# One sum of the transform's first pass made by accumulating DMA transfers instead of VectorE

## The chip, the core and the metric

The kernel runs on one core of a Trainium2 chip. Its time is in device microseconds (us); the median of three runs stands for it. The engines are TensorE (PE in the profile), VectorE (DVE), ScalarE (ACT), GpSimd (POOL) and SyncE (SP). SP issues most transfers, ACT some stores; before the change POOL issues none.

## The reference

Four layers with residuals: two Fourier mixing layers and two attention layers with a memory. Only the first Fourier layer is touched here:

```python
a = jnp.einsum("bsd,ed->bse", x, dft_hid_re)
b = jnp.einsum("bsd,ed->bse", x, dft_hid_im)
y = jnp.einsum("ts,bse->bte", dft_seq_re, a) - jnp.einsum("ts,bse->bte", dft_seq_im, b)
...
x = x + _A_ref(_layernorm(x, axis=-1), A_dft_seq_re, A_dft_seq_im, A_dft_hid_re, A_dft_hid_im)
x = x + _B_ref(_layernorm(x, axis=-1), B_wq, B_wk, B_wv, B_wo, B_beta)
```

The sequence has 2048 rows of 512 features, all in float32. The kernel applies the sequence matrices first and the hidden ones after.

## The kernel before

**Tiling.** The 2048 output rows are four chunks (`tcn`, 0 to 3) of 512. The input rows are sixteen tiles of 128, taken in pairs (tile `k` and tile `k + 8`), so a chunk has eight steps, `k` = 0 to 7. For each chunk and step the array `ct` holds four 128x512 blocks of the sequence matrices, beside one another: the second and the first half of the real matrix, then the first and the second half of the imaginary one.

**Passes.** Chunk 0 goes the plain way (`contract`). Chunks 1 to 3 replace eight block products by seven, P1 to P7, of sums of blocks. A first pass runs P1, P2, P7 and P4 for chunks 1, 2 and 3, step by step, the four products in turn; a second pass runs P6, P5 and P3. Every float32 operand is split into a high and a low part, and each product is three matmuls (`matmul3`); with two output tiles a product's step is six matmuls, which the program calls a slot. A step of the first pass is four slots. When a product has run its eight steps, its two accumulators are read out into `c` (line 497 on ACT, line 499 on DVE).

**The step's operands** come from `read_all` (line 381), a generator placed at five slots ahead of the step's own slot `t`: -11, -6, -4, -2, -1. It takes two homes of 128x2x512 (`re` and `im`), fetches the four blocks into them, and makes three sums on DVE, one after another. With `re[0]`, `re[1]`, `im[0]`, `im[1]` the blocks in order:

- line 386: `im[0]` + `im[1]` replaces `im[0]`; it is P7's operand
- line 387: `re[1]` + the new `im[0]` replaces `im[1]`; it is stored in DRAM for the second pass (line 397, by ACT)
- line 390: `re[0]` + the new `im[1]` replaces `re[0]`, once `rights` has split the old `re`; it is P4's operand

The splits are lines 96 (ACT, the high part `chi`) and 98 (DVE, the low part `clo`). `chi` and `clo` have three buffers each, so a split waits until TensorE is through with an older one.

**Homes.** `raw_pair` hands out nine homes: four in `cring`, two in `craw`, three in `v_all`; always the one released longest ago. A step uses two. `release` only orders the program: on the chip a fetch into a home waits for the last reader of its old content, which for `im` is the store of line 397.

**Order.** Instructions keep their program order on TensorE; on DVE the sums are pinned to it (`pin`) and the rest is placed by a scheduler, which also orders SP's, ACT's and POOL's queues. Each engine runs its queue in order. `read_rest` (the second pass) is placed by slots too; its subtraction is line 409. `join_rows` changes the left operands (`xa`) between the passes.

Of the kernel before, what the change touches and what calls it, by code (L numbers as in the profile page):

```python
# [14 lines left out]
ALU = mybir.AluOpType  # L15
# [41 lines left out]
def spectral_infini_kernel(  # L57
# [13 lines left out]
    V, A, G, T = nc.vector, nc.scalar, nc.gpsimd, nc.tensor  # L71
# [18 lines left out]
    pin = tc.keep_in_program_order  # L90

    def split(hi, lo, src, scale=1.0, lo_engine=V, hi_engine=None):
        if hi_engine is V:
            return V.tensor_copy(hi, src), V.tensor_tensor(out=lo, in0=src, in1=hi.bitcast(F32), op=ALU.subtract)
        else:
            pin(A.activation(hi, src, AF.Copy, scale=scale))  # L96
        if scale == 1.0:
            lo_engine.tensor_tensor(out=lo, in0=src, in1=hi.bitcast(F32), op=ALU.subtract)  # L98
        else:
            V.scalar_tensor_tensor(  # L100
                lo, src, scale, hi.bitcast(F32), op0=ALU.mult, op1=ALU.subtract
            )
# [12 lines left out]
    def pair(name, tag, bufs, dtype=F32R):  # L115
        return sb.tile([P, 2, 512], dtype, name=name, tag=tag, bufs=bufs)
# [67 lines left out]
    def place(order, gen, *at):  # L184
        for t in itertools.chain(*at):
            slots.setdefault(t, []).append((order, gen))

    def run_from(t, n, step=1):
        return range(t, t + n * step, step)
# [14 lines left out]
    def place_spectral(x_in, x_out, t0, end, ln_at, direct):  # L204
# [69 lines left out]
        def change_rows(k):  # L274
            two, j = raw_pair()
            new = two[:, 0, : D // 2]
            fetch(new, joined[k][:, 0])
            yield
            replace(k, slice(D // 2, D), new)
            release(j)  # L280
            yield
# [34 lines left out]
        def raw_pair(own=False):  # L316
            clock[0] += 1
            if not homes:
                ring = sb.tile([P, 2 * LT, 512], F32, name="cring", tag="xT", bufs=1)
                homes.extend(ring[:, j : j + 2] for j in range(0, 2 * LT, 2))  # L320
                if direct:
                    homes.extend(pair("craw", "craw", 2, F32) for _ in range(2))
                    homes.extend(spare[:, j : j + 2] for j in range(0, 6, 2))
            elif not direct and len(homes) == LT and clock[0] > 24:
                homes.extend(pair("craw", "craw", 2, F32) for _ in range(2))
            j = min((j for j in range(LT if own else len(homes)) if released.get(j, 0) is not None), key=lambda j: released.get(j, 0))
            released[j] = None
            return homes[j], j

        def release(*held):  # L330
            for j in held:
                clock[0] += 1
                released[j] = clock[0]

        def rights(src):
            hi, lo = pair("chi", "chi", 3), pair("clo", "clo", 3)
            split(hi, lo, src)
            return [(hi[:, j], lo[:, j]) for j in range(2)]
# [8 lines left out]
        def fetch(dst, src):  # L347
            with tc.issue_after(last_stack[0].ins) if last_stack[0] else nullcontext():
                nc.sync.dma_start(dst, src)
# [31 lines left out]
        def read_all(tcn, k):  # L381
            (re, j), (im, n) = raw_pair(), raw_pair()
            fetch(re, ct[tcn, k, :, :2])
            fetch(im, ct[tcn, k, :, 2:])
            yield
            pin(V.tensor_tensor(out=im[:, 0], in0=im[:, 0], in1=im[:, 1], op=ALU.add))
            later.append(pin(V.tensor_tensor(out=im[:, 1], in0=re[:, 1], in1=im[:, 0], op=ALU.add)))
            yield
            right[tcn, "P2", k], right[tcn, "P1", k] = rights(re)
            pin(V.tensor_tensor(out=re[:, 0], in0=re[:, 0], in1=im[:, 1], op=ALU.add))  # L390
            yield
            hi, lo = pair("chi", "chi", 3), pair("clo", "clo", 3)
            split(hi[:, 0], lo[:, 0], im[:, 0])
            split(hi[:, 1], lo[:, 1], re[:, 0])
            right[tcn, "P7", k], right[tcn, "P4", k] = ((hi[:, h], lo[:, h]) for h in range(2))
            yield
            nc.scalar.dma_start(sums[tcn, k][:, 1], im[:, 1])
            release(j, n)
            yield
# [49 lines left out]
        def contract(tcn):  # L449
            ps = [[bank(f"u{d}") for d in range(DT)] for _ in range(2)]  # L450
            for k in range(HALF):
                for h2 in range(2):
                    for cc in range(2):
                        parts = right[tcn, cc, h2, k]
                        for d in range(DT):
                            matmul3(
                                ps[cc][d],
                                lambda h: xa[k + HALF * h2][:, h, d * P : (d + 1) * P],
                                lambda h: parts[h],
                                (k, h2) == (0, 0),  # L460
                                (k, h2) == (HALF - 1, 1),
                            )
                        if (k, h2, cc) != (HALF - 1, 1, 1):
                            yield
            for cc in range(2):
                for d in range(DT):
                    if d % 2 == 0:
                        block(tcn, (d // 2, cc))
                    dst = c[tcn, (d // 2, cc)][:, d % 2]
                    if cc == 0:  # L470
                        A.activation(dst, ps[cc][d], AF.Copy)
                    else:
                        V.tensor_scalar(dst, ps[cc][d], -1.0, None, op0=ALU.mult)
            yield
# [106 lines left out]
        t = start  # L581
        if direct:
            place(2, contract(0), run_from(t, 4 * HALF, 2))
            for k in range(HALF):
                place(3, read_plain(0, k), [t + 8 * k + d for d in (-12, -4, 1, 4)])
                place(3, change_rows(k), [t + 8 * k + d for d in (5, 9)])
            t += 8 * HALF
            names = "P1", "P2", "P7", "P4"
            for tcn in range(1, TC):
                for n, name in enumerate(names):  # L590
                    place(2, product(tcn, name), run_from(t + n, HALF, 4))
                for k in range(HALF):
                    place(3, read_all(tcn, k), [t + 4 * k + d for d in (-11, -6, -4, -2, -1)])
                t += 4 * HALF
            for k in range(HALF):
                place(3, join_rows(k), [t + 5 * k + d for d in (-33, -27)])
            for tcn in range(1, TC):
                for n, name in enumerate(CHAIN):
                    place(2, product(tcn, name), run_from(t + n, HALF, 3))
                for k in range(0, HALF, 2):  # L600
                    place(3, read_rest(tcn, k), [t + 3 * k + d for d in (-12, -6, -3, 0)])
                t += 3 * HALF
        else:
            for names in ("P1", "P7"), ("P2", "P4"):
                for tcn in range(TC):
                    for n, name in enumerate(names):
                        place(2, product(tcn, name), run_from(t + n, HALF, 2))
                    for k in range(HALF):
                        place(3, read_pair(tcn, k, names), [t + 2 * k + d for d in (-10, -6, -4, -3)])
                    t += 2 * HALF  # L610
            for k in range(HALF):
                place(3, add_rows(k), [t - 48 + 6 * k, t - 44 + 6 * k])
            for tcns in (0, 1), (2, 3):
                at = {tcn: [] for tcn in tcns}
                for name, tcn in itertools.product(CHAIN, tcns):
                    at[tcn] += run_from(t, HALF)
                    for k in range(0, HALF, 2):
                        place(3, read_two(tcn, k, name), [t + k + d for d in (-9, -4, -3)])
                    t += HALF
                for tcn in tcns:  # L620
                    place(2, chained(tcn), at[tcn])
        for k in range(2 * DT):
            cc, d = k // DT, k % DT
            tag = "craw" if k < 2 else ("chi", "clo")[k % 2]
            t = end - 7 + k if k < 2 else end - 3 + (k - 2) // 2
# [675 lines left out]
```

## Time and profile before

| | |
|---|---|
| median of 3 runs | 1825.14 us |
| lowest, highest | 1822.15, 1827.36 us |
| the profiled execution | 1827.82 us |
| its span | 1825.6 us |
| granted TensorE clock over the span | 0.991 |
| first pass, chunks 1 to 3 | 98 to about 230 us |
| second pass | to 338 us |
| runs of lines 386, 387, 390 | 24 each |

In the profile, PE is TensorE's matmuls and PEld its weight loads, which overlap. A row of a timeline starts with when an instruction began and how long it took; in brackets stands how long its engine had been idle and what ended that. `cring<-in_ct` is a transfer from `ct` into a home of the ring. The profiled execution's time has some 2 us more than its span.

### The profile page before, as it was taken

The page shows a single profiled execution, that of the slowest core. Times are in us where ns is not written, and L with a number is a line of the kernel's source. Part 1 is how long each engine was busy: PE and PEld are TensorE (multiplying, and loading weights), DVE is VectorE, ACT ScalarE, POOL GpSimd, SP SyncE. Part 2 cuts the span into 40 slices and gives each one's busy share as a digit, 9 for nine tenths or more (in the row PEclk, how much of TensorE's full clock was granted, in tenths as well). Part 3 has the DMA queues.
Part 4 walks back from the last instruction along what each step waited for, and adds up shares of the span by engine and source line. Part 5 has one row for each costly group of instructions (what it writes and reads, how often), then busy time and mean ns, then how long its engine had stood idle before and what let it go on. Part 6 is the DMA issues. An engine that isn't in the chain of part 4 may idle for free.

```text
span 1825.6 us, 32144 instructions
## 1 busy us (share of the span) xinstructions
PE 1752.3 (96%) x10192; PEld 1263.1 (69%) x10192; DVE 1417.2 (78%) x4240; ACT 1095.1 (60%) x2359; POOL 493.7 (27%) x805
## 2 busy tenths in 40 slices
PE   8999999999999999999899999999998999999998
PEld 6888777877556665665568787888875666666655
DVE  8888977764877978878877898667658778787785
ACT  3344443432987877777764444444428887877785
POOL 1000000013443444354531000000134443544442
PEclk9999999999999999999999999999999999999999
DMA  8777765355443534433565666544545434344341
GB/s 285 252 265 234 248 218 176 115 179 163 157 134 97 165 115 132 140 124 117 170 193 197 204 226 230 196 162 133 169 144 175 134 119 156 114 134 142 107 127 44
DMA packets 168345, 300.70 MB, mean 165 GB/s; under 512 B 19440, under 2 KB 70640, under 8 KB 168176
## 3 DMA queue, kind: packets, MB, share of 16 engines
q1 hardware_dynamic: 158000, 285.29, 48.3%
q10 hardware_dynamic: 10176, 13.37, 2.0%
q8 instruction: 80, 1.31, 0.3%
q14 instruction: 89, 0.73, 0.1%
HBM read 209.73 MB, written 88.08 MB: 163 GB/s over the span
## 4 chain that ended last, share of the span: by engine, by line
PE 68%; DVE 12%; DMA 4%; issue 3%; ACT 2%; POOL 1%; SPq 0%; DVEq 0%; ACTq 0%; POOLq 0%
PE m L82 17%; PE pqk L82 9%; PE y L82 8%; PE pv_bank L82 7%; PE sT L82 7%; PE nat L82 6%; PE pvv L82 4%; PE po L82 4%; DVE junk L791 3%; DMA stkk<-scrk 1%; DVE c L499 1%; DVE clo L98 1%; PE pm L82 1%; PE on L82 1%; PE pM L82 1%
## 5 line engine op out<-in xcount | busy, mean ns | idle before, releaser
L791 DVE CUSTOM_DVE_ANT_0 junk<-nat,mask 128x512 bf16<-128x512 f32 (+3 forms) x1024 | 496.7, 485 | 159.6 <-PE nat L82 124.4
L860 ACT ACTIVATE pT<-sT 128x512 f32<-128x512 f32 x640 | 371.8, 599 | 14.9 <-DVE sT L857 1.4
L863 POOL TENSOR_SCALAR_AFFINE_SELECT pT<-pT 128x256 f32<-128x256 f32 (+1 forms) x448 | 203.2, 467 | 474.1 <-ACT pT L860 376.9
L82 PE MATMUL m<-chi,xa 128*128 128x512 f32 x1056 | 310.3, 394 | 3.7 <-DVE c L499 2.1
L82 PE MATMUL nat<-stkk,stkq 96*128 96x512 bf16 (+3 forms) x1024 | 246.3, 302 | 10.2 <-DVE mx L791 6.7
L82 PE MATMUL sT<-stkq,stkk 99*128 99x256 bf16 (+3 forms) x1024 | 250.2, 306 | 4.4 <-ACT pT L860 1.8
L82 PE MATMUL m<-clo,xa 128*128 128x512 f32 x720 | 235.1, 398 | 7.4 <-DVE clo L98 7.4
L859 ACT ACTIVATE sT<-sT 128x256 f32<-128x256 f32 (+1 forms) x628 | 205.0, 336 | 51.8 <-PE sT L82 49.3
L82 PEld LDWEIGHTS m<-chi,xa 128*128 128x128 f32 x1056 | 199.2, 189 | 47.1 <-DVE c L499 2.9
L82 PE MATMUL y<-wdt,us 128*128 128x512 f32 x768 | 182.3, 391 | 0.2 <-DVE wdt L98 0.2
L82 PEld LDWEIGHTS <-stkk 99*128 99x128 bf16 x1024 | 81.9, 98 | 132.8 <-issue 120.5
L82 PEld LDWEIGHTS m<-clo,xa 128*128 128x128 f32 x720 | 135.7, 190 | 42.0 <-DVE clo L98 14.5
L82 PEld LDWEIGHTS y<-wdt,us 128*128 128x128 f32 x768 | 143.5, 188 | 30.4 <-DVE wdt L98 0.9
L82 PE MATMUL pv_bank<-pT,v_all 128*17 128x512 f32 (+3 forms) x2048 | 154.7, 440 | 1.1 <-POOL pT L863 1.1
L96 ACT ACTIVATE chi<-cring 128x512 fp32r<-128x512 f32 (+1 forms) x137 | 99.1, 727 | 90.4 <-PE m L82 41.3
L145 POOL TENSOR_TENSOR r<-ve,half_neg 128x2 f32<-128x2 f32 (+2 forms) x24 | 19.9, 828 | 451.5 <-DVE ve L143 448.7
L82 PEld LDWEIGHTS <-stkq 96*128 96x128 bf16 x1024 | 94.6, 99 | 64.5 <-issue 21.8
L82 PE MATMUL pvv<-wv,xT 128*128 128x512 f32 x384 | 127.3, 443 | 3.6 <-DVE mx L791 3.6
L82 PE MATMUL pqk<-xT,wq 128*128 128x512 f32 x384 | 129.9, 448 | 0.0
L82 PE MATMUL po<-wo,oh 128*128 128x512 f32 x384 | 123.6, 438 | 3.1 <-DVE mx L791 2.2
L82 PE MATMUL pqk<-xT,wk 128*128 128x512 f32 x384 | 123.4, 430 | 0.0
L82 PEld LDWEIGHTS pv_bank<-pT,v_all 128*17 128x17 f32 x2048 | 53.5, 98 | 90.2 <-issue 85.1
(187 smaller groups left out, 3003.6 us busy)
## 6 DMA issues: line engine op xcount, KB each, us to landing
cring<-sum SPq DMA_DIRECT2D x105, 256.0 KB
stkq<-scrq SPq DMA_DIRECT2D x64, 384.0 KB
stkk<-scrk SPq DMA_DIRECT2D x64, 384.0 KB
cring<-in_ct SPq DMA_DIRECT2D x80, 256.0 KB
xt<-mid SPq DMA_DIRECT2D x64, 256.0 KB
cring<-in_ct SPq DMA_DIRECT2D x27, 512.0 KB
mid<-xr SPq DMA_DIRECT2D x48, 256.0 KB
scrq<-parts SPq DMA_DIRECT2D x32, 384.0 KB
```

The costliest lines, as they stand in the source:

```text
L82: return tc.keep_in_program_order(op(*args, **kwargs))
L96: pin(A.activation(hi, src, AF.Copy, scale=scale))
L98: lo_engine.tensor_tensor(out=lo, in0=src, in1=hi.bitcast(F32), op=ALU.subtract)
L145: G.tensor_tensor(out=r, in0=ve, in1=half_neg[:, :n], op=ALU.pow)
L499: V.tensor_tensor(out=dst, in0=c[tcn, base][:, m], in1=ps[m], op=op)
L791: last_max[0] = V.tensor_tensor_reduce(junk[:, :n], src, mask[:, 512 - n :], 1.0, 3e38, ALU.add, ALU.min, dst,)
L859: A.activation(blocks, blocks, AF.Relu)
L860: A.activation(dst, ps, AF.Exp, scale=-SCALE)
L863: G.affine_select(blocks, blocks, pattern=[[0, n] for n in blocks.shape[1:-1]] + [[1, P]], compare_op=ALU.is_ge, fill=0.0, base=0, channel ...
```

## The change

From step 2 of chunk 1 on (22 of the 24 steps) the first sum is no longer made by DVE. SP fetches only `im[0]` (256 KB instead of 512), and POOL issues a second transfer that reads the last block from DRAM and adds it to `im[0]` in place. The first two steps keep the old way. `read_all` gets one slot more and starts two slots earlier: -13 fetch, -9 POOL's transfer, -6 sums, -4, -2, -1.

```diff
         def read_all(tcn, k):
             (re, j), (im, n) = raw_pair(), raw_pair()
             fetch(re, ct[tcn, k, :, :2])
-            fetch(im, ct[tcn, k, :, 2:])
-            yield
-            pin(V.tensor_tensor(out=im[:, 0], in0=im[:, 0], in1=im[:, 1], op=ALU.add))
+            early = (tcn, k) < (1, 2)
+            fetch(im if early else im[:, 0], ct[tcn, k, :, 2:] if early else ct[tcn, k, :, 2])
+            yield
+            if not early:
+                G.dma_start(im[:, 0], ct[tcn, k, :, 3], accum_op=ALU.add)
+            yield
+            if early:
+                pin(V.tensor_tensor(out=im[:, 0], in0=im[:, 0], in1=im[:, 1], op=ALU.add))
             later.append(pin(V.tensor_tensor(out=im[:, 1], in0=re[:, 1], in1=im[:, 0], op=ALU.add)))
...
                 for k in range(HALF):
-                    place(3, read_all(tcn, k), [t + 4 * k + d for d in (-11, -6, -4, -2, -1)])
+                    place(3, read_all(tcn, k), [t + 4 * k + d for d in (-13, -9, -6, -4, -2, -1)])
```

Line numbers below the change grow by five: the second sum is line 392 after it, the third 395, the read-outs 504, the second pass's subtraction 414.

DVE's queue inside the first pass, before the change: two steps of chunk 1, each with its sums in lines 386, 387 and 390.

```order
L386 TENSOR_TENSOR cring<-cring 128x512
L387 TENSOR_TENSOR cring<-v_all,cring 128x512
L98 TENSOR_TENSOR clo<-cring,chi 128x512
L390 TENSOR_TENSOR v_all<-v_all,cring 128x512
L98 TENSOR_TENSOR clo<-craw,chi 128x1024
L98 TENSOR_TENSOR clo<-v_all,chi 128x512
L386 TENSOR_TENSOR cring<-cring 128x512
L387 TENSOR_TENSOR cring<-craw,cring 128x512
```

The same place after it, two steps:

```order
L392 TENSOR_TENSOR cring<-cring 128x512
L98 TENSOR_TENSOR clo<-cring,chi 128x1024
L395 TENSOR_TENSOR cring<-cring 128x512
L98 TENSOR_TENSOR clo<-cring,chi 128x512 x2
L392 TENSOR_TENSOR craw<-cring,craw 128x512
L98 TENSOR_TENSOR clo<-cring,chi 128x1024
L395 TENSOR_TENSOR cring<-cring,craw 128x512
```

The first sum is gone, and a step's wide split (128x1024, P1 and P2) stands behind the second sum (line 392), which now waits for POOL's transfer.

POOL's queue after the change, from the row statistics of chunk 0 (line 145) to the ones of the values (line 1256); before it, these two stand next to each other.

```order
L145 TENSOR_TENSOR r<-ve,half_neg 128x2 x7
L388 DMA cring<-in_ct 128x512
L388 DMA craw<-in_ct 128x512
L388 DMA v_all<-in_ct 128x512
L388 DMA cring<-in_ct 128x512
L388 DMA craw<-in_ct 128x512
L388 DMA v_all<-in_ct 128x512 x2
L388 DMA cring<-in_ct 128x512 x3
L388 DMA craw<-in_ct 128x512
...
L1256 MEMSET v_all 128x32 x6
```

POOL's new rows are the accumulating transfers alone; nothing of its own stands between them.

DVE's queue where the first pass ends and the second begins, before the change: the last sum (line 390), the read-outs (line 499) and the second pass's first subtractions (line 409).

```order
L390 TENSOR_TENSOR cring<-cring,v_all 128x512
L499 TENSOR_TENSOR c<-c,m_1723 128x512
L98 TENSOR_TENSOR clo<-cring,chi 128x512
L409 TENSOR_TENSOR cring<-cring 128x512
L409 TENSOR_TENSOR v_all<-v_all,cring 128x512
L499 TENSOR_TENSOR c<-c,m_1724 128x512
L499 TENSOR_TENSOR c<-c,m_1733 128x512
```

The same place after it:

```order
L395 TENSOR_TENSOR cring<-cring 128x512
L98 TENSOR_TENSOR clo<-cring,chi 128x512 x2
L414 TENSOR_TENSOR v_all<-v_all,craw 128x512 x2
L504 TENSOR_TENSOR c<-c,m_1726 128x512
L98 TENSOR_TENSOR clo<-v_all,chi 128x1024
L504 TENSOR_TENSOR c<-c,m_1727 128x512
```

The last split and the two subtractions have moved ahead of the first read-out. TensorE's order of matmuls is unchanged.

## The prediction

> **What bounds the kernel now.** I read the page first, then the busy time of each engine by windows over the first transform, then the timelines of TensorE, DVE, SP and ACT there.
>
> ```profile
> span 1825.6 us, 32144 instructions
> PE 1752.3 (96%) x10192; PEld 1263.1 (69%) x10192; DVE 1417.2 (78%) x4240; ACT 1095.1 (60%) x2359; POOL 493.7 (27%) x805
> ...
> PE 68%; DVE 12%; DMA 4%; issue 3%; ACT 2%; POOL 1%; SPq 0%; DVEq 0%; ACTq 0%; POOLq 0%
> ```
>
> TensorE (PE) is busy for 96% of the span and holds 68% of the chain of waits. DVE, from which the change takes work, holds 12%. So a faster DVE is worth only what TensorE loses to it near the change. Lines 386 to 390 run only in the first transform:
>
> ```profile
> core 0: us, PE busy (x) PEld busy (x) DVE busy (x) ACT busy (x) POOL busy (x), PEclk, DMA share, GB/s
> 98.00:229.00 131.00, 129.10 (x564) 105.17 (x563) 114.39 (x164) 58.26 (x86) 0.00 (x0) 1.00 0.75 249
> 229.00:338.00 109.00, 104.75 (x449) 84.48 (x448) 84.73 (x109) 45.09 (x53) 0.65 (x6) 0.98 0.54 178
> ...
> 141.50:152.40 10.90, 10.09 (x45) 8.00 (x44) 10.57 (x17) 4.04 (x6) 0.00 (x0) 1.00 0.70 241
> 152.40:163.30 10.90, 10.90 (x50) 9.04 (x49) 9.02 (x13) 4.62 (x7) 0.00 (x0) 1.00 0.73 243
> ...
> 228.70:240.00 11.30, 9.42 (x35) 7.24 (x34) 10.88 (x16) 5.51 (x8) 0.00 (x0) 0.85 0.67 206
> ```
>
> The columns are the stretch, its length, busy time and instructions of PE, weight loads, DVE, ACT and POOL, then granted clock, DMA share and GB/s. 98 to 229 us is the first pass (four products for chunks 1 to 3), 229 to 338 us the second pass. In the first pass TensorE idles 131.00 - 129.10 = 1.9 us, DVE is busy 114.39 of 131 us (87%), POOL not at all. An ordinary stretch (152.40 to 163.30) has TensorE full and DVE at 9.02 of 10.90; only where a chunk ends and its accumulators are read out (141.50 to 152.40) does DVE fill (10.57) and TensorE fall short (10.09). Where the passes meet, TensorE gets 9.42 of 11.30 us at a clock of 0.85.
>
> ```profile
> 98.16 0.39 PE L82 MATMUL m<-chi,xa 128*128 128x512 f32 x1
> ...
> 108.13 0.62 PE L82 MATMUL m<-chi,xa 128*128 128x512 f32 x2
> ...
> 110.85 0.62 PE L82 MATMUL m<-chi,xa 128*128 128x512 f32 x2
> ...
> 146.96 0.51 PE L82 MATMUL m<-clo,xa 128*128 128x512 f32 x1 [0.81 <-DVE clo L98]
> ...
> 234.59 0.50 PE L82 MATMUL m<-clo,xa 128*128 128x512 f32 x1 [1.88 <-DVE clo L98]
> ...
> 337.95 4.28 PE L82 MATMUL y<-wdt,us 128*128 128x512 f32 x18
> ```
>
> Rows start with start and duration. The matmuls of this form follow each other in threes, 0.68 us apart: twelve from 108.13 to 110.85 is 2.72 / 12 = 0.2267 us each. The two passes hold 3 chunks x 7 products x 8 steps x 6 = 1008 of them, 228.5 us at that pitch; they take 337.95 - 98.16 = 239.8 us. All that TensorE loses in both passes is 11.3 us, 0.6% of the span: the ceiling of any gain here. The two waits shown (0.81 and 1.88 us) both end on a DVE split.
>
> **The change part by part.** *Removed*: line 386 in 22 of its 24 runs.
>
> ```profile
> L386 DVE TENSOR_TENSOR cring<-cring x11: 683/685/689, 92.5 to 214.0; 128x512 f32<-128x512 f32 x11
> L386 DVE TENSOR_TENSOR v_all<-v_all x8: 683/686/689, 106.7 to 225.4; 128x512 f32<-128x512 f32 x8
> L386 DVE TENSOR_TENSOR craw<-craw x5: 682/685/685, 112.1 to 207.1; 128x512 f32<-128x512 f32 x5
> ...
> 112.14 0.69 DVE L386 TENSOR_TENSOR craw<-craw 128x512 f32<-128x512 f32 x1
> 112.86 0.69 DVE L387 TENSOR_TENSOR craw<-v_all,craw 128x512 f32<-128x512 f32 x1
> 113.57 0.69 DVE L98 TENSOR_TENSOR clo<-craw,chi 128x512 fp32r<-128x512 f32 x1
> 114.18 0.68 DVE L390 TENSOR_TENSOR v_all<-v_all,craw 128x512 f32<-128x512 f32 x1
> 115.82 1.83 DVE L98 TENSOR_TENSOR clo<-v_all,chi 128x1024 fp32r<-128x1024 f32 x2 [0.96 <-ACT chi L96]
> ```
>
> One lasts 0.685 us, and the next DVE instruction starts 0.60 to 0.72 us after it, so 22 free 22 x 0.6 = 13 us or more of DVE in the first pass, about 0.6 us in every step. A step is 24 matmuls, 24 x 0.2267 = 5.44 us; DVE's work there falls from 4.5 us (9.02 / 2) to 3.9.
>
> Most of this buys nothing: before 115.82 DVE waits 0.96 us for ACT's part of the split, and that for TensorE to give a buffer back. DVE already runs as far ahead as the buffers let it. It buys time in the two chunk ends inside the pass, and where the passes meet.
>
> Term 1, inside the first pass: at most the 1.9 us idle, which the waits of TensorE there put on DVE's splits (total, times, longest):
>
> ```profile
> PE m L82 <- DVE clo L98: 1.9, 3, 0.8
> ```
>
> In 141.50 to 152.40 two adds go (1.2 us), more than the 0.81 us that TensorE lost there. I take 1.5 us.
>
> Term 2, where the passes meet. The chain of waits there, and DVE:
>
> ```profile
> 214.17 14.85 PE m L82 x62
> 229.02 0.03 issue
> ...
> 229.12 0.43 DVE c L499
> ...
> 229.72 0.68 DVE clo L98
> 230.41 0.60 DVE cring L409
> 231.01 0.60 DVE v_all L409
> 231.61 1.25 DVE c L499 x3
> ```
>
> DVE waits for the read-out at 229.12, then has a split, two subtractions of line 409 and more read-outs in front of what TensorE needs at 234.59. In the changed order the split and both subtractions stand ahead of the first read-out: 3 x 0.6 = 1.8 us leave this queue, as much as TensorE's 1.88 us wait. There is room for them, since chunk 3's eight removed adds free 4.8 us before 229. With the wait would go the clock dip that follows it (0.85 over 11.3 us, 1.7 us). I take both, 3.6 us; nothing if the clock dips anyway and line 409's data come late.
>
> *Added*: 22 accumulating transfers of 256 KB, issued by POOL, which has no row between 98 and 229 us and delays nobody. They cost DMA time and a second trip in series. No transfer of this kind is in the trace, so both are bounded.
>
> DMA time: 0.75 of the engines at 249 GB/s means 332 GB/s when full, so one pass of 256 KB is 0.262 MB / 332 GB/s = 0.79 us of all sixteen. The block is fetched from HBM as before; added is at least a read of the destination, one pass. A step uses 0.75 x 5.44 = 4.08 us of DMA; with one pass 4.87 (share 0.90), and it is full at 1 + 1.36 / 0.79 = 2.7 passes of the accumulating transfer.
>
> Landing time, from the nearest rows:
>
> ```profile
> 0.80 0.38 SPq L120 DMA_DIRECT2D xt<-in_x  x1
> 3.32 0.69 DVE L132 BATCH_NORM_STATS2 st<-xt 128x6 f32<-128x512 f32 x1 [3.32 <-DMA xt<-in_x]
> ...
> 108.13 0.33 ACTq L397 DMA_DIRECT2D sum<-v_all  x1
> ...
> 102.71 0.33 SPq L349 DMA_DIRECT2D craw<-in_ct  x1
> 115.18 0.33 SPq L349 DMA_DIRECT2D v_all<-in_ct  x1
> 126.01 0.43 SPq L349 DMA_DIRECT2D v_all<-in_ct  x1
> ```
>
> The first 256 KB load, on an empty queue, is used 3.32 - 0.80 = 2.5 us after its issue. The 256 KB store issued by ACT at 108.13 is what SP's fetch at 115.18 waits for (it takes the store's buffer): 7.0 us, amid a burst of fetches. So 2.5 to 7.0 us. I take 5, nearer the busy end: the share here is 0.75, but POOL's queue holds nothing else. The Trainium skill, "DMA: Bandwidth & Descriptors", section "Anatomy of one DMA — SWDGE (gpsimd) path", fits 2.0 us plus bytes over 436 GB/s for a transfer issued by GpSimd; by it this one would take an estimated 2.6 us. The sum would stay, and the late landing among the rivals would fall to a chance of about 0.05; the store's 7.0 us in this very stretch keeps me from it.
>
> Is there room? The fetch of chunk 1's step 3 is issued at 102.71; its first add starts at 112.14 and line 387, which now waits for the transfer, at 112.86. That is 10.1 us for fetch and accumulation, the tightest I found. A 256 KB fetch of about 3 us and 5 us make 8: hidden, though at the bad end (7 + 7) it would be 4 us late. Behind line 387 on DVE's queue wait the step's splits, and TensorE for those. That step begins on TensorE at 98.16 + 3 x 5.44 = 114.48; P7's split ends at 113.57 + 0.69 = 114.26 and is used two slots (2.72 us) into the step, 2.9 us later; P4's ends at 115.82 + 1.83 = 117.65, used three slots in, 0.9 us later, 1.5 without the removed add. I take no cost, with the bad ends kept for the range.
>
> *Moved*: the fetch is put two slots earlier (a slot is 6 matmuls, 1.36 us), but what holds it is the buffer:
>
> ```profile
> SPq L349 <- DMA sum<-v_all: 40.7, 7, 7.3
> SPq L349 <- DMA sum<-cring: 34.2, 9, 7.5
> SPq L349 <- DMA sum<-craw: 28.5, 5, 7.0
> ```
>
> In 97 to 232 us SP's fetches wait 40.7 + 34.2 + 28.5 = 103 us for stores to free their homes. So the early slots shift little after the first steps, and each home is held for the same work. The order of matmuls is the same. No cost.
>
> Sum: 1.5 + 3.6 = 5.1 us. The profiled execution took 1827.82 us (span 1825.6 and 2.2 around it), 2.7 above the runs' median: 1827.8 - 5.1 - 2.7 = **1820 us**.
>
> **The rivals.** *DMA becomes the bound* (slower). If reading, adding and writing back take four passes, a step needs 4.08 + 3 x 0.79 = 6.45 us of DMA against 5.44 of TensorE: 22 x 1.01 = 22 us, 1847 us. It decides from 2.7 passes on; at 3 it costs 22 x 0.22 = 5 us, 1830. For it: the share is already 0.75, in places more. Against: a read of the destination is one pass, and the engines stand a quarter free. The Trainium skill, "DMA: Bandwidth & Descriptors", section "Issuing engines are not separate DMA queues", has all issuers share the same sixteen engines; by it POOL's empty queue brings no bandwidth, and this rival gets 0.17 where I would give 0.10 otherwise.
>
> *The transfer lands late* (slower). The nine homes serve 4.5 steps, 24.5 us. Store 7.0, fetch 7, accumulation A, and 0.7 from line 387 to its store make 14.7 + A; beyond A = 9.8 us the ring sets the pace. At A = 12, 2.2 us per turn, 22 / 4.5 turns: 11 us, 1836 us. For it: 7.0 us stores. Against: needs more than the worst row.
>
> *DVE's relief does not arrive* (no change). The clock dips anyway and the read-outs still bunch: term 1 alone, 1823 or 1824 us. For it: the read-outs themselves stay on DVE (four rows of line 499 above).
>
> *Not what it says*: POOL generates descriptors late, so that the adds wait for POOL rather than for data. It would read as the second rival with a smaller price, and POOL is empty: in that one's chance.
>
> **How the numbers follow.** Forecast 0.58, DMA bound 0.17, late landing 0.14, no relief 0.11. The forecast's own range is 1814 (all 11.3 us) to 1823 (term 1). A measurement of this kernel tells about 0.3%, 5.5 us, from no change: the forecast stands at that edge, 0.40 faster beyond it and 0.18 within; no relief gives 0.02 faster, 0.07 within and 0.02 slower; the other two give 0.30 slower and 0.01 within. Faster 0.42, within 0.26, slower 0.32. The range, 1813 to 1838 us, takes in the late landing and the three-pass case and leaves out the four-pass end.
>
> **What would show it.** Right: 22 accumulating transfers on a queue of POOL's, two rows of the old add left, the wait at 147 gone, the passes meeting without a wait near 234 us and the clock there near 1; 1008 matmuls in about 235 us. Wrong: DVE idle ahead of line 387 (392 in the new code) with a transfer as releaser, DMA share near 1 in the first pass, or matmuls over 240 us. A change of time outside 95 to 340 us would mean that I looked in the wrong place.

## The result, and the profile after

The changed kernel takes 1830.71 us (median of 19 runs, 1823.75 to 1834.28); the kernel before, run beside it, 1825.04 us (19 runs, 1818.12 to 1829.31). The ratio is 1.0031 with a 95% interval of 1.0019 to 1.0042: 0.3% slower, some 5.7 us. 1820 us had been forecast. The profiled execution of the changed kernel took 1828.06 us, 2.65 below its median, that of the kernel before lay 2.7 above the median of its own three runs, so their spans differ by less than the medians. The page of the changed kernel, its span, its engines and its chain of waits by engine:

```profile
span 1826.3 us, 32183 instructions
PE 1750.6 (96%) x10192; PEld 1261.9 (69%) x10192; DVE 1401.9 (77%) x4218; ACT 1095.5 (60%) x2359; POOL 513.1 (28%) x827
...
PE 70%; DVE 15%; DMA 7%; issue 4%; ACT 2%; POOL 1%; SPq 0%; DVEq 0%; ACTq 0%; POOLq 0%
```

DVE lost 15.3 us of work (1417.2 to 1401.9), as planned; yet in the chain that ended last DVE went from 12 to 15% and transfers from 4 to 7%. Where, the windows tell (the same columns as before):

```profile
98.00:229.00 131.00, 124.44 (x535) 100.89 (x534) 94.38 (x134) 54.33 (x78) 19.29 (x22) 0.98 0.87 247
229.00:338.00 109.00, 106.63 (x452) 86.14 (x452) 84.59 (x107) 45.77 (x52) 0.65 (x6) 0.97 0.55 178
108.80:119.70 10.90, 8.20 (x36) 6.42 (x35) 4.36 (x7) 3.37 (x5) 2.92 (x4) 0.97 1.02 311
119.20:122.60 3.40, 3.40 (x9) 2.63 (x8) 3.14 (x5) 1.54 (x3) 0.00 (x0) 0.51 1.02 175
122.60:130.60 8.00, 8.00 (x37) 6.62 (x36) 5.71 (x8) 2.89 (x6) 0.87 (x1) 1.00 0.84 228
217.80:228.70 10.90, 8.35 (x35) 6.34 (x34) 5.67 (x9) 3.04 (x5) 1.72 (x2) 0.98 0.96 289
228.40:231.70 3.30, 3.30 (x8) 2.61 (x9) 3.20 (x7) 1.92 (x3) 0.00 (x0) 0.50 0.83 216
231.70:240.00 8.30, 8.30 (x38) 6.77 (x37) 7.68 (x13) 4.86 (x8) 0.00 (x0) 0.99 0.80 243
279.30:282.80 3.50, 3.50 (x10) 2.68 (x10) 2.84 (x5) 1.06 (x1) 0.00 (x0) 0.54 0.68 243
```

In the first pass TensorE is busy 124.44 of 131 us, where it had 129.10, at a clock of 0.98 instead of 1.00. Two stretches carry the loss: 108.80 to 119.70 and 217.80 to 228.70, each with some 2.6 us of TensorE idle, the DMA share at 1.02 and 0.96 (as it is recorded it can pass 1) and DVE itself half idle (4.36 and 5.67 of 10.90). Behind each, TensorE is full, but for some 3.4 us at half clock (0.51 and 0.50), about 1.7 us of work lost each time; then the clock is back at 1. A third such stretch, at 279.30, lies in the second pass. TensorE's timeline (start, duration, and in brackets the idle time ahead and what ended it):

```profile
98.54 0.39 PE L82 MATMUL m<-chi,xa 128*128 128x512 f32 x1
...
117.95 0.50 PE L82 MATMUL m<-clo,xa 128*128 128x512 f32 x1 [2.70 <-DVE clo L98]
...
151.40 0.50 PE L82 MATMUL m<-clo,xa 128*128 128x512 f32 x1 [0.29 <-DVE clo L98]
...
228.27 0.72 PE L82 MATMUL m<-clo,xa 128*128 128x512 f32 x1 [2.48 <-DVE clo L98]
...
279.07 0.50 PE L82 MATMUL m<-chi,xa 128*128 128x512 f32 x1 [1.60 <-DVE c L504]
...
344.11 1.07 PE L82 MATMUL y<-wdt,us 128*128 128x512 f32 x4
```

The two passes last 344.11 - 98.54 = 245.6 us, against 239.8 before: the 5.8 us more are the whole of the difference between the medians. The waits that the change was to relieve did shrink: 0.81 us at 146.96 is now 0.29 at 151.40, and the 1.88 us at 234.59, where the passes meet, is gone. Two new ones are larger than both, 2.70 and 2.48 us, and again the releaser is a split of DVE. The wait of 1.60 us for a read-out isn't new. The kernel before has it too, there without a loss of clock:

```profile
274.52 0.50 PE L82 MATMUL m<-chi,xa 128*128 128x512 f32 x1 [1.60 <-DVE c L499]
```

```profile
274.50:278.00 3.50, 3.48 (x15) 2.91 (x16) 2.84 (x5) 1.06 (x1) 0.00 (x0) 1.00 0.68 229
```

DVE's timeline ahead of the wait of 2.70 us:

```profile
109.67 0.69 DVE L98 TENSOR_TENSOR clo<-craw,chi 128x512 fp32r<-128x512 f32 x1 [0.70 <-ACT chi L96]
116.06 0.69 DVE L392 TENSOR_TENSOR craw<-v_all,craw 128x512 f32<-128x512 f32 x1 [5.71 <-DMA craw<-in_ct]
116.67 1.22 DVE L98 TENSOR_TENSOR clo<-v_all,chi 128x1024 fp32r<-128x1024 f32 x1
```

and the sums of its waits for transfers from 97 to 232 us (total, times, longest):

```profile
DVE craw L392 <- DMA craw<-in_ct: 11.0, 3, 5.7
DVE v_all L392 <- DMA v_all<-in_ct: 4.2, 2, 3.8
```

Line 392 is the first add that remains on DVE, and the first reader of the accumulated sum. At 116.06 it had stood idle for 5.71 us, for the transfer into `craw`. In all it waits 15.2 us in five places; before, it waited for no transfer. The chain of waits goes further back (start, duration, what):

```profile
96.58 7.07 DMA sum<-craw
...
103.67 2.80 DMA craw<-in_ct
...
108.24 7.80 DMA craw<-in_ct
...
206.07 7.75 DMA sum<-cring
...
214.81 6.13 DMA craw<-in_ct
...
221.60 4.76 DMA craw<-in_ct
...
226.99 1.23 DVE clo L98
```

Read it as three trips in a row. A store of a finished sum takes 7.07 us, and SP's queue stands behind it, so the fetch into its home goes out only at 103.67, two slots early or not. The accumulating transfer is issued 4.6 us later, at 108.24, and lands after another 7.80 us. Near the end of chunk 3 it is 7.75, 6.13 and 4.76 us: there the accumulation itself is no slower than elsewhere, but the two trips ahead of it are. Only behind the third trip can DVE make the step's splits.

### The profile page after: what moved, and what is told of

It is laid out like the page before. It is cut to its first block, busy times and chain, and to the rows that moved or that the text cites. A ratio compares the mean times of both kernels' runs of the same rounds, so it can differ in the third digit from the quotient of the medians.

```text
span 1826.3 us, 32183 instructions
## 1 busy us (share of the span) xinstructions
PE 1750.6 (96%) x10192; PEld 1261.9 (69%) x10192; DVE 1401.9 (77%) x4218; ACT 1095.5 (60%) x2359; POOL 513.1 (28%) x827
## 3 DMA queue, kind: packets, MB, share of 16 engines
q0 software_dynamic: 3168, 5.77, 1.9%
## 4 chain that ended last, share of the span: by engine, by line
PE 70%; DVE 15%; DMA 7%; issue 4%; ACT 2%; POOL 1%; SPq 0%; DVEq 0%; ACTq 0%; POOLq 0%
PE m L82 19%; PE pqk L82 9%; PE y L82 8%; PE pv_bank L82 8%; PE sT L82 7%; PE nat L82 6%; PE pvv L82 4%; PE po L82 4%; DVE junk L796 3%; DVE clo L98 2%; DVE c L504 2%; DMA craw<-in_ct 1%; PE pm L82 1%; PE on L82 1%; PE pM L82 1%
## 5 line engine op out<-in xcount | busy, mean ns | idle before, releaser
L82 PEld LDWEIGHTS <-stkq 96*128 96x128 bf16 x1024 | 94.3, 99 | 64.2 <-issue 22.5
```

What stands on the lines that cost most here:

```text
L82: return tc.keep_in_program_order(op(*args, **kwargs))
```

## The experiments

The theory: the sum is now made by a second trip that must wait for the first; where transfers are slow, the trip ends after DVE needs it, and TensorE waits. Against it stood, first, that the extra passes of the DMA engines slow everything, whoever waits; second, that only the start is late; third, that DVE's relief was worth nothing. All twelve runs at a glance: the ratio to the kernel before on the same chip, the length of the two passes in the one profile of each, the time that DVE waits from 97 to 232 us for a transfer ahead of the first add that it makes, and the DMA share from 98 to 229 us.

| run | ratio [95%] | passes, us | DVE waits, us | DMA share |
|---|---|---|---|---|
| before | 1 | 239.8 | 0 | 0.75 |
| changed | 1.0031 [1.0019, 1.0042] | 245.6 | 15.2 | 0.87 |
| e1, add left out | 0.9988 [0.9972, 1.0004] | 237.2 | 0 | 0.77 |
| e2, DVE adds through step 3 | 1.0030 [1.0010, 1.0050] | 246.3 | 18.9 | 0.86 |
| e3, DVE adds at both ends | 1.0017 [1.0002, 1.0033] | 242.8 | 13.2 | 0.87 |
| e4, plain second trip | 0.9999 [0.9988, 1.0011] | 236.7 | 8.3 | 0.80 |
| e5, one tile aside | 1.0128 [1.0103, 1.0154] | 260.1 | 0 | 0.75 |
| e6, early slots only | 1.0009 [0.9993, 1.0026] | 240.7 | 0 | 0.76 |
| e7, summed block first | 1.0036 [1.0021, 1.0051] | 243.0 | 19.4 | 0.88 |
| e8, sum on GpSimd | 0.9992 [0.9974, 1.0010] | 236.8 | 0 | 0.77 |
| e9, three tiles aside | 0.9983 [0.9964, 1.0003] | 234.2 | 0.5 | 0.89 |
| e10, chunk ends only | 1.0001 [0.9985, 1.0018] | 238.9 | 0.9 | 0.82 |
| e11, two sums on GpSimd | 1.0031 [1.0015, 1.0048] | 243.3 | 0 | 0.76 |
| e12, plain trip and load | 1.0032 [1.0014, 1.0050] | 246.3 | 22.5 | 0.86 |

The medians have 12 runs each (6 for e5); a single profile of the passes can lie 3 us off what its ratio says (e7), in part because a stretch of half clock (1.7 us) appears in one profile and not in another. In e1, e4, e5, e9 and e12 the first sum is left out, so they price the change and aren't versions of it.

**e1: the add left out.** What is the relief alone worth? The kernel before, with

```diff
-            pin(V.tensor_tensor(out=im[:, 0], in0=im[:, 0], in1=im[:, 1], op=ALU.add))
+            if (tcn, k) < (1, 2):
+                pin(V.tensor_tensor(out=im[:, 0], in0=im[:, 0], in1=im[:, 1], op=ALU.add))
```

> The kernel before, with the first sum left out in the 22 steps and nothing in its place (P7, the stored sums and P4 lack the last imaginary block there). It prices DVE's relief alone. Theory (two late landings cost more than the relief brings): the first transform's two passes take 3 to 5 us less than before (239.8 us from the first m matmul to the first y matmul), and the time is 1820 to 1822 us. Rival (the relief is worth nothing, TensorE being full): within 1 us of before.

The passes fall by 2.6 us, and TensorE no longer waits where they meet; the ratio's interval just includes 1. The relief is real, with 2.6 us in this profile instead of the forecast's 5.1.

**e2 and e3: fewer transfers.** If only the start is late, leaving the first steps or both ends to DVE should mend it.

```diff
-            early = (tcn, k) < (1, 2)
+            early = (tcn, k) < (1, 4)                    # e2
+            early = not (1, 4) <= (tcn, k) < (3, 5)      # e3
```

> The change, with the first sum left on DVE for chunk 1's steps 2 and 3 as well (20 accumulating transfers). Theory (late landing at chunk 1's step 3 costs 4.4 us with the clock dip behind it): DVE's wait there and TensorE's 2.70 us are gone, the passes take about 241 us instead of 245.6, the time is about 4 us under the change's. Rival (the extra DMA pass is the cost): the wait only moves to the next step that accumulates, 245 us stay.

> The change, with accumulating transfers only from chunk 1's step 4 to chunk 3's step 4 (17 of them); the other seven sums on DVE. Theory: both late landings (chunk 1 step 3, chunk 3 step 6) are gone, the passes take 237 to 240 us, the time is equal to the kernel before's or up to 3 us better. Rival (extra DMA pass): DMA share stays near 0.85 and new waits on transfers appear in the middle, 243 us or more.

In e2 the wait at step 3 is gone and six others come, 1.1 to 4.4 us long: 18.9 us in all, passes of 246.3 us. The theory of a late start fails. e3 leaves 13.2 us of waits in the middle of the pass and 1.0017. The lateness follows the transfers; it isn't a matter of one place.

**e4: the same trip as a plain copy.**

```diff
-                G.dma_start(im[:, 0], ct[tcn, k, :, 3], accum_op=ALU.add)
+                G.dma_start(im[:, 0], ct[tcn, k, :, 3])
```

> The change, with POOL's 22 transfers plain copies: they overwrite the first imaginary block instead of adding to it, so the sum is left out. Same trips in series, one DMA pass fewer per trip. Theory (what counts is that a second trip starts only when the fetch has landed): the trip shortens by 1 to 3 us from 5.5 to 7.7 us, chunk 1's step 3 still waits 3 to 5 us, the passes take 243 to 245 us. Rival (the second pass of the accumulation is the cost): no DVE wait for a transfer, 236 to 239 us.

With the two trips still in a row, DVE waits 8.3 us, and almost nothing is lost by it (TensorE waits 1.15 us at 222.60): 236.7 us, no slower than e1. So a second trip by itself is not the price. The queue row (packets, MB, share of 16 engines over the span) of the changed kernel, with the us from issue to landing of its 22 transfers,

```profile
q0 software_dynamic: 3168, 5.77, 1.9%
...
DMA to landing us min/median/max: 4.3/6.6/8.4
```

and of e4,

```profile
q0 software_dynamic: 1760, 5.77, 1.1%
...
DMA to landing us min/median/max: 3.8/5.4/7.6
```

show what accumulation adds: 3168 / 22 = 144 packets a transfer for 80, and 1826.3 x 0.019 / 22 = 1.58 us of all engines for 1823.9 x 0.011 / 22 = 0.91 us. A landing takes 6.6 us in the median, against 5.4 in e4. GpSimd's own time for the issue hardly varies (0.85 to 0.89 us in all but the first, 1.05), so the rows give no sign that GpSimd is late. Two readings were left: the additional load slows everything, or it only makes the awaited transfer later.

**e5 and e9: nobody waits.** To part them, the accumulating transfers stay, at the same places, and go to a tile aside; DVE adds without waiting for them.

```diff
-                G.dma_start(im[:, 0], ct[tcn, k, :, 3], accum_op=ALU.add)
...
+                G.tensor_copy(aside[0][:, :1], im[:, 0, :1])
+                G.dma_start(aside[0], ct[tcn, k, :, 3], accum_op=ALU.add)
```

> The changed kernel with the same 22 accumulating transfers at the same places, but into a tile that nobody reads: a one-column copy on GpSimd waits for the fetch and for the last transfer, then the transfer is issued; the adds of DVE no longer wait for it. The first sum is left out in these 22 steps. If the waiting for late transfers is what costs, the first pass and the second (first m to first y matmul) take about 237 us, as with the add left out, at a DMA share of 0.87. If the load on the DMA engines costs by itself (fetches, stores and output blocks that come later), they stay at 243 to 246 us. In between, the difference to 237 is the load's price, and that to 245.6 the waiting's.

This missed its purpose: 260.1 us, slower than any. GpSimd's timeline shows why:

```profile
124.30 0.29 POOL L391 COPY rem<-cring 128x1 f32<-128x1 f32 x1 [7.03 <-DMA rem<-in_ct]
124.95 0.90 POOL L392 DMA_DIRECT2D rem<-in_ct  x1 [0.36 <-POOL rem L391]
```

With one tile the copy waits for the transfer before it (7.03 us in the brackets), so the transfers fall behind the steps; the copy also reads the home, which is therefore freed late, and SP's fetches waited for that copy (total, times, longest, 97 to 340 us):

```profile
SPq L349 <- POOL rem L391: 83.2, 14, 7.9
```

It tells of a chain that the experiment itself made, not of the change. e9 takes three tiles in turn, with the wait for the fetch apart from them (`k % 3` picks the tile; `aside[3]` is a one-column tile, `seen` in the profile, that stands between):

```diff
-                G.dma_start(im[:, 0], ct[tcn, k, :, 3], accum_op=ALU.add)
...
+                G.tensor_copy(aside[3], im[:, 0, :1])
+                G.tensor_tensor(out=aside[k % 3][:, :1], in0=aside[3], in1=aside[3], op=ALU.subtract)
+                G.dma_start(aside[k % 3], ct[tcn, k, :, 3], accum_op=ALU.add)
```

> Again the changed kernel with its 22 accumulating transfers going to tiles that nobody reads, now three tiles in turn, so that a transfer waits for the fetch of its own step and not for the transfer before it (in the run with one tile that chain let the transfers go only every 7.7 us, which held the buffers). The first sum is left out in these 22 steps. If waiting for late transfers is the price, first m to first y matmul falls from 245.6 to about 237 us and no matmul waits 2.7 us for a split; if the load on the DMA engines delays the fetches themselves, 243 us or more, with waits of the splits on fetches.

The same loads and stores, the same order of TensorE, DVE and ACT as the changed kernel, and transfers that land about as slowly (6.3 us in the median, against 6.6): the passes take 234.2 us, the least of all. Its windows:

```profile
98.00:229.00 131.00, 130.34 (x571) 106.65 (x571) 103.08 (x147) 60.11 (x89) 35.65 (x66) 1.00 0.89 253
118.00:129.00 11.00, 11.00 (x50) 9.13 (x49) 7.75 (x11) 4.43 (x6) 3.27 (x7) 1.00 1.07 323
```

all that DVE waits for a transfer there (97 to 232 us),

```profile
DVE craw L399 <- DMA craw<-in_ct: 0.5, 1, 0.5
```

The fetch for chunk 1's step 3 goes out at 104.67 there, and GpSimd's copy that waits for it begins at 108.69, 4.0 us later. In the changed kernel the chain puts the issue at 108.24 on DVE's add of the step before; such a fetch would end at 103.67 + 4.0 = 107.7, about as late, so that the issue need not have waited for DVE.

At a DMA share of 0.89 over the pass, and 1.07 in a stretch of it, TensorE is busy 130.34 of 131 us at full clock. The load alone costs nothing here. Waiting for the late transfers costs 245.6 - 234.2 = 11.4 us. TensorE's waits for DVE's splits from 98 to 345 us, of the changed kernel and of e9, give one half of it:

```profile
PE m L82 <- DVE clo L98: 6.8, 6, 2.7
```

```profile
PE m L82 <- DVE clo L98: 0.9, 3, 0.3
```

That is 6.8 - 0.9 = 5.9 us. The granted clock gives the other: the three stretches of half clock, 1.7 + 1.7 + 1.6 = 5 us, where e9 has none (1.00, and 1.00 from 229 to 338 us). Not all of this belongs to late transfers. The third stretch follows the wait of 1.60 us that the kernel before has as well. Without it 11.4 becomes 9.8 us, and the medians say 1.0031 - 0.9983 = 0.0048, some 9 us.

**e12: a plain trip, and load beside it.** The opposite cut: DVE waits for a plain copy, and a second copy of the same block goes to the tiles aside.

```diff
-                G.dma_start(im[:, 0], ct[tcn, k, :, 3], accum_op=ALU.add)
...
+                G.tensor_copy(aside[3], im[:, 0, :1])
+                G.tensor_tensor(out=aside[k % 3][:, :1], in0=aside[3], in1=aside[3], op=ALU.subtract)
+                G.dma_start(aside[k % 3], ct[tcn, k, :, 3])
+                G.dma_start(im[:, 0], ct[tcn, k, :, 3])
```

> The changed kernel with plain copies by GpSimd in place of the accumulating transfers, and behind each a second plain copy of the same block into a tile that nobody reads: 2 x 0.91 us of all DMA engines in each step against 1.58 us with accumulation and 0.91 us with one copy. The first sum is left out. If load on the DMA engines makes the change slow, the passes go from 236.7 us (one copy) to 243 us or more, as with accumulation, at a share near 0.87. If it is the accumulating transfer's own slowness, they stay at 237 to 239 us.

In the program the awaited copy (line 396) stands last; on GpSimd's queue the scheduler has put it ahead of the other (line 395):

```profile
108.29 0.56 POOL L396 DMA_DIRECT2D craw<-in_ct  x1
108.85 0.55 POOL L395 DMA_DIRECT2D rem<-in_ct  x1
```

The share is 0.86, as with accumulation, and so is the time: 1.0032, passes of 246.3 us. DVE's waits (line 400 is its first add there, 97 to 232 us),

```profile
DVE v_all L400 <- DMA v_all<-in_ct: 11.8, 3, 5.0
DVE craw L400 <- DMA craw<-in_ct: 10.7, 3, 4.9
```

and the largest on TensorE's timeline:

```profile
229.53 0.79 PE L82 MATMUL m<-clo,xa 128*128 128x512 f32 x1 [2.88 <-DVE clo L98]
```

Together, e4, e9 and e12 show the cause. A wait for a second trip without the load (e4) and the load without the wait (e9) cost nothing; the two together cost as much where the awaited transfer copies (e12, 246.3) as where it accumulates (changed, 245.6). The clock, which dips in some of these profiles and not in others behind the same wait of 1.60 us, doesn't make the difference: without it, by TensorE's idle time in the passes alone (their length less its busy time), it is 8.9 us in the changed kernel and 10.1 in e12, for 3.0 in e9, 4.6 in e4 and 6.2 before. At chunk 1's step 3 the add begins 5.9 us after the awaited transfer's issue in e4, 6.8 in e12 and 7.8 in the changed kernel. One thing in e12 isn't the load: two small GpSimd instructions stand ahead of each issue, and at this step it goes out 0.5 us later in the passes than in e4. So that adding on the way costs nothing beyond its second pass is likely, but not shown to the microsecond.

**e6 and e7: the parts around it.** e6 is the kernel before with the change's early fetch slot:

```diff
-                    place(3, read_all(tcn, k), [t + 4 * k + d for d in (-11, -6, -4, -2, -1)])
+                    place(3, read_all(tcn, k), [t + 4 * k + d for d in (-13, -6, -4, -2, -1)])
```

> The kernel before with the first pass's fetches placed two slots earlier, as the change has them, and nothing else. The prediction gave this part no cost: first m to first y matmul about 240 us, time within 0.1% of before. Rival: the earlier fetches crowd the stores, so that the passes take 242 us or more and part of the change's loss comes from here.

No difference that can be told: 240.7 us, and a ratio about 1. e7 fetches the block that is accumulated into ahead of the others:

```diff
-            fetch(re, ct[tcn, k, :, :2])
             early = (tcn, k) < (1, 2)
             fetch(im if early else im[:, 0], ct[tcn, k, :, 2:] if early else ct[tcn, k, :, 2])
+            fetch(re, ct[tcn, k, :, :2])
```

> The changed kernel with the block that is accumulated into fetched ahead of the step's two other blocks, not behind them. If the order of the two trips in a row is what makes them late, the accumulation starts 1 to 3 us earlier, the waits of DVE ahead of its first add (5.7, 3.8 and 4.5 us) shrink by as much, and the passes come down from 245.6 to about 242 us, 1827 us in all. If the DMA engines are short of time at those places, the two other blocks land later in its place: waits of the same sum on other blocks, passes of 244 to 246 us.

The passes are 2.5 us shorter in its profile and the largest waits a little smaller (4.9, 4.8), but DVE waits more in all (19.4 us) and the time does not come down: 1.0036. A start that is earlier by one transfer is lost again in the crowd; whether it gains a microsecond stays open.

**e10: the ends of chunks only.**

```diff
-            early = (tcn, k) < (1, 2)
+            early = (tcn, k) not in ((1, 7), (2, 0), (2, 1), (2, 7), (3, 0), (3, 1))
```

> The changed kernel with only 6 transfers in place of 22: in the last step of a chunk and the first two of the next, where DVE also reads out eight banks; the other steps add on DVE as before. If DVE's relief is worth something only there and each further transfer only costs, the wait before 234.6 us stays away, no wait near 118 us appears, and the passes take 238 us. Rival: the transfers of these places are late too, since loads and stores crowd there as well: a wait of 2 us or more before a split after 140 or 180 us, passes of 240 us or more.

Six transfers are not late (0.9 us of waits), at a share of 0.82, and there is no loss. There is no gain either: the wait of 1.88 us at 234.85 stayed, against what was expected, because the steps that precede it (the last of chunk 3) weren't among the six.

**e8 and e11: the sum on GpSimd.** The relief without any transfer:

```diff
-            pin(V.tensor_tensor(out=im[:, 0], in0=im[:, 0], in1=im[:, 1], op=ALU.add))
+            pin((V if (tcn, k) < (1, 2) else G).tensor_tensor(out=im[:, 0], in0=im[:, 0], in1=im[:, 1], op=ALU.add))
```

> The kernel before with the sum of the same 22 steps made by GpSimd, by a vector add of 128x512 (1.2 us by the rows of such adds elsewhere in the profile), and no accumulating transfer. If relief of DVE without load on the DMA engines and without a second trip is worth what leaving out the add was worth, the passes take 237 to 238 us, 0.15% faster than before. Rival: the handover from GpSimd (1.2 us and a semaphore, with DVE's next add queued right behind) stalls DVE, or the two engines slow each other: passes of 240 us or more and waits of DVE on GpSimd of over 1 us each.

The passes take 236.8 us, as with the add left out. The ratio 0.9992 (0.9974 to 1.0010) can't be told from 1. e11 gives GpSimd the second pass's subtraction of line 409 as well:

```diff
-                pin(V.tensor_tensor(out=x[h][:, 0], in0=x[h][:, 1], in1=y[:, h], op=ALU.subtract))
+                pin(G.tensor_tensor(out=x[h][:, 0], in0=x[h][:, 1], in1=y[:, h], op=ALU.subtract))
```

> The kernel before with the first pass's sum of the same 22 steps and also the second pass's subtraction (line 409, two per double step) made by GpSimd. If what GpSimd takes off DVE is gained wherever read-outs crowd DVE, the passes fall from 236.8 (first pass alone) to about 235 us, by the wait of 1.6 us before a matmul in the second pass. Rival: adds of DVE that run beside an add of GpSimd take 1.78 instead of 0.68 us, so the second pass gains nothing: 236 to 238 us.

That is 0.3% slower, beyond the rival's price. The wait of 1.60 us ahead of the second pass's read-outs shrank to 0.46, and many of 0.4 to 1.4 us came. GpSimd's timeline of e8, and DVE's beside it, show a reason:

```profile
109.33 1.29 POOL L386 TENSOR_TENSOR craw<-craw 128x512 f32<-128x512 f32 x1 [12.51 <-DMA craw<-in_ct]
111.90 2.15 POOL L386 TENSOR_TENSOR cring<-cring 128x512 f32<-128x512 f32 x1 [1.28 <-DVE craw L387]
```

```profile
109.79 1.39 DVE L98 TENSOR_TENSOR clo<-cring,chi 128x512 fp32r<-128x512 f32 x1 [0.70 <-ACT chi L96]
111.09 0.68 DVE L387 TENSOR_TENSOR craw<-v_all,craw 128x512 f32<-128x512 f32 x1
111.70 1.21 DVE L98 TENSOR_TENSOR clo<-v_all,chi 128x1024 fp32r<-128x1024 f32 x1
112.94 1.66 DVE L390 TENSOR_TENSOR v_all<-v_all,craw 128x512 f32<-128x512 f32 x1
```

A DVE operation of 0.68 us takes 1.39 or 1.66 where GpSimd had begun an add, and GpSimd's add 2.15 where DVE had begun a split (111.70, its usual 1.21), 1.29 at best: as these rows stand, one ends before the other gets on. What DVE is spared it partly pays back.

No version was found that beats the kernel before by more than can be told; of those that make every sum, e8 is the nearest.

## Why the prediction was wrong

- **The bound** (TensorE with 11.3 us to lose in the two passes) was right, and the ceiling held: the best run, e9, leaves 5.7 us of it.
- **Terms 1 and 2** (DVE's relief, 5.1 us) were right in kind. The two waits named went or shrank as said. In size, the runs that keep the relief and drop the late transfers give 239.8 - 237.2 = 2.6 us (e1) to 239.8 - 234.2 = 5.6 us (e9); their ratios give 2 to 3 us.
- **The load of the transfers** was right: one pass more each (1.58 us of all engines, 2 x 0.79), a share of 0.87 where 0.90 was forecast, and e9 shows that it costs nothing by itself. The rival by which DMA becomes the bound falls.
- **The moved fetch** was right to cost nothing (e6), and for the reason given: SP stands behind stores, and the fetch for step 3 left at 103.67 instead of 102.71.
- **"Two trips hidden at no cost" failed.** The step took a fetch of about 3 us and A = 5 us for 10.1 us of room. At chunk 1's step 3, 4.6 us pass from the first fetch's issue to the accumulation's, and A is 7.8, against a worst row of 7.0: 12.4 us from 103.67 to 116.06, 3.2 us behind the 112.86 of the kernel before. The prediction had written down 4 us late as its bad end, and then took A below its worst row, because the mean share was 0.75 and GpSimd's queue otherwise empty. But where it was late the share was 1.02 and 0.96. The Trainium skill, "DMA: Bandwidth & Descriptors", section "Anatomy of one DMA — SWDGE (gpsimd) path", has a fit by which the prediction estimated 2.6 us; the traces don't agree, with a median of 6.6 us in this pass.
- **The slack behind the transfer** failed too: it was read off the old order. The prediction counted 2.9 us from P7's split to its use and 0.9 from P4's (1.5 without the add). But the wide split of P1 and P2, whose use is the second matmul of the step, now stands behind line 392. In the kernel before it ran ahead of the step's sums (112.14 and 112.86 for step 3):

```profile
110.39 1.23 DVE L98 TENSOR_TENSOR clo<-v_all,chi 128x1024 fp32r<-128x1024 f32 x1 [0.90 <-ACT chi L96]
```

  In e4, with the new order:

```profile
113.56 0.69 DVE L392 TENSOR_TENSOR craw<-v_all,craw 128x512 f32<-128x512 f32 x1 [2.75 <-DMA craw<-in_ct]
114.17 1.22 DVE L98 TENSOR_TENSOR clo<-v_all,chi 128x1024 fp32r<-128x1024 f32 x1
```

  There the split ends at 115.39. The step begins on TensorE at 98.99 + 3 x 5.44 = 115.31, its second matmul 0.23 us later: some 0.15 us of slack, not 0.9. So at this step e4's transfer came just in time, and whatever lands later holds TensorE up. In the changed kernel the split ends at 117.89 and TensorE goes on at 117.95. What the same lateness would cost with this split ahead of the sum again, no run shows.
- **What lateness costs** was put down as a ring that sets the pace (A beyond 9.8 us; 1836 us). It costs earlier and otherwise: A of 7.8 us at one step stalls TensorE for 2.70 us, and the clock then stands at half for 3.4 us, 1.7 us more. The sum that should have stood there is 11.4 us, against a relief of 5.6: +5.8. Of the 11.4, 1.6 us are the stretch at 279.30, behind a wait that no transfer made. Against the kernel before, TensorE idles 8.9 - 6.2 = 2.7 us more, and the clock, with three such stretches for one, brings the rest.

The time, 1830.7 us, lies inside the range; the sign of the likeliest case was the wrong one.

## What to carry to other kernels

Taking an operation off an engine by a transfer that adds on the way puts a second trip in series with the first; price it by the slowest landings in the stretch where the buffer comes free last, and not by the mean share. Before trusting such a change, ask of each end apart, what the load costs with nobody waiting and what the wait costs without the load: here both were free, and only the two together cost 0.3%. Read the slack behind the transfer off the new order of the waiting engine's queue, not the old one. An engine that idles beside a busy one isn't free help either, if the two slow each other.

## What the runs showed of the hardware

- After TensorE waits of 2.70 and 2.48 us the granted clock stood at 0.51 and 0.50 for some 3.4 us, though TensorE was then full, and after that at 1.00 and 0.99: each wait was paid for with 1.7 us more. It isn't so behind every wait: one of 1.60 us was followed by 0.54 in the changed kernel (279.30) and by 1.00 in the kernel before (274.50). The Trainium skill, "TensorE: Matmul & The Clock Gate", section "Part 1: The HAM clock gate (the "warmup" mystery)", has the clock fall to half after an idle window of some 3.4 us and come back after a busy one as long. The length of the dips agrees; the waits that brought them, 1.60 to 2.70 us, were shorter than that window.
- A 256 KB transfer that accumulates took 144 packets and 1.58 us of the 16 engines, a plain copy 80 and 0.91. GpSimd was busy 0.88 us with the issue of the one (19.29 us for 22) and 0.56 us with the other (12.27 us for 22).
- DVE and GpSimd, each with float32 adds of 128x512 side by side, took 1.66 us for 0.68 and 2.15 for 1.29 in the rows of e8 above. The Trainium skill, "GPSIMD Engine Reference", section "Specifications", has GpSimd share its SBUF interfaces with VectorE, with contention where a DVE instruction has two inputs in SBUF; these rows agree.
- With the DMA engines at a share of 0.89 over 131 us TensorE was busy for 130.34 of them, as long as no instruction of DVE stood behind the added transfers (e9).
